# Transposing x, q and k of batches 2 to 4 by DMA instead of on TensorE, in a fused attention and mixing kernel

## The chip, the cores and the metric

One NeuronCore of a Trainium2 chip. The time is device microseconds (us) of one execution. TensorE multiplies matrices, VectorE (DVE in the profile) and ScalarE (ACT) work element by element, GpSimd (POOL) does the same more slowly, SyncE (SP) only issues transfers. All transfers go through 16 DMA engines that the issuers share. An execution counts as slow when it is over 1.5% above the fastest of its kernel. Ratios below use fast runs alone, with a 95% interval.

## The reference

```python
# q, k, v: (4 batches, 8 heads, 768 tokens, 64), f32; heads 0, 2 and 6 are "retrieval" heads
scores = q @ k.T / 8
# retrieval heads: causal mask; the others: 4 first tokens, and a window of 64 tokens
a = softmax(where(mask, scores, -1e9))
x = (a @ v).transpose(0, 2, 1, 3).reshape(4, 768, 512)
theta = x @ w_theta
zr, zi = x * cos(theta), x * sin(theta)
y = w_tok_r @ zr + w_tok_i @ zi          # mixes the tokens, per batch
u = x + y
out = u + maximum(u @ w_ch, 0)
```

## The kernel before

Matrix products run in bf16. Three operands have to be turned so that the contracted axis lies on the partitions: q and k (head dimension) before the scores, and x (channels) before theta. Before the change TensorE turns all of them: two heads at a time into a PSUM tile, from which a copy takes them to SBUF. The copies also order the tokens, because a partition of the loaded tile holds six neighbouring tokens.

```python
def load_qk(what, b, heads):             # f32 in DRAM, bf16 in SBUF: a casting load, issued by POOL
    if (what, b) not in state:
        state[what, b] = two.tile([128, H, NB * D], BF16, tag=f"{what}b", name=f"{what}b")
    src = {"q": q, "k": k}[what][b].rearrange("h (p j) d -> p h (j d)", p=128)
    nc.gpsimd.dma_start(out=state[what, b][:, heads], in_=src[:, heads])

def load_v(b, n, after=None):            # not cast: issued by SP, in two halves per pair of heads
    ...
    for x, h in enumerate(PAIRS[n]):
        nc.sync.dma_start(out=t[:, x], in_=src[:, h])

def turn_qk(what, b, n):                 # 12 transposes: 6 token blocks of 2 heads
    pt = state["pt", what, n] = ps_x.tile([128, 1024], BF16, tag="x", name="pt")
    for j in range(NB):
        for x, h in enumerate(PAIRS[n]):
            nc.tensor.transpose(pt[64 * x:64 * x + 64, j * 128:(j + 1) * 128], state[what, b][:, h, j * D:(j + 1) * D], ident)

def keep_qk(eng, what, n):               # PSUM to SBUF, tokens ordered
    o = dst.rearrange("d (p j) -> d p j", j=NB)
    i = state.pop(("pt", what, n))[:, :S].rearrange("d (j p) -> d p j", j=NB)
    ...

def turn_x(b, i):                        # 4 transposes of a 128-token tile of x; keep_x copies them out
    ...
```

The order of instructions on every engine is not the order of the code. A small planner holds a list of steps, each with an engine, an estimated duration and what it depends on. It simulates them and emits every engine's queue in the simulated order. A transfer is a step with an estimated landing time:

```python
tp = add("PE", 340, lambda ...: turn_qk(what, b, n), [landed[what, b, n]], take="x", mode="64c")
kept[what, b, n] = add("ACT" if act else "DVE", 720 if act else 900, lambda ...: keep_qk(...), [tp] + old, give=[tp])
...
issue = add("SP", 1500, lambda b=b, n=n: load_v(b, n), [cast[b - 1, n], xk[b - 1, 5]], take="st_v")
land = add("DMA", 2000, None, [issue])
```

On the chip each queue runs strictly in that order. A step whose input is late holds up all that stands behind it, needed or not. Batches are counted from 1 in the text and from 0 in the code.

The softmax here doesn't subtract the row's maximum and nothing guards it: scores larger than these inputs give would overflow.

Of the kernel before, what the change touches and what calls it, by code (L numbers as in the profile page):

```python
# [10 lines left out]
BF16 = mybir.dt.bfloat16  # L11
# [6 lines left out]
PAIRS = [(0, 2), (4, 6), (1, 3), (5, 7)]  # L18
# [13 lines left out]
class Plan:  # L32
# [5 lines left out]

    LATENCY = {"PE": (230, 0), "ACT": (190, 60), "DVE": (120, 60), "POOL": (150, 60), "SP": (50, 0), "DMA": (2000, 0)}
    SWITCH = {"PE": 95, "ACT": 1300}  # L40
# [13 lines left out]
    def order(self, free):  # L54
# [4 lines left out]
        rank = {}  # L59
# [21 lines left out]
        while events:  # L81
# [8 lines left out]
            for e in engines:  # L90
# [3 lines left out]
                for s in ready.get(e, ()):  # L94
                    if ready_at[id(s)] > now or (s.take and slots[s.take] < 1):
                        continue
                    value = -ready_at[id(s)] if e == "DMA" else rank[id(s)] + s.bias
                    if s.mode and s.mode != mode.get(e):
                        value -= self.HOLD.get(e, 0)
                    if best is None or value > best[0]:  # L100
                        best = (value, s)
# [32 lines left out]
def kernel(  # L134
# [28 lines left out]
    two = ctx.enter_context(tc.tile_pool(name="two", bufs=2))  # L163
    stage = ctx.enter_context(tc.tile_pool(name="stage", bufs=4))
    work = ctx.enter_context(tc.tile_pool(name="work", bufs=2))
# [28 lines left out]
    state = {}  # L194
    plan = Plan({"s": 2, "m": 2, "x": 2, "u": 4, "uT": 3, "ot": 2, "ct": 2, "st": 2, "wtok": 4, "st_v": 4})
    add = plan.add
# [7 lines left out]
    def load_qk(what, b, heads):  # L204
        if (what, b) not in state:
            state[what, b] = two.tile([128, H, NB * D], BF16, tag=f"{what}b", name=f"{what}b")
        src = {"q": q, "k": k}[what][b].rearrange("h (p j) d -> p h (j d)", p=128)
        nc.gpsimd.dma_start(out=state[what, b][:, heads], in_=src[:, heads])
# [38 lines left out]
    def turn_qk(what, b, n):  # L247
        pt = state["pt", what, n] = ps_x.tile([128, 1024], BF16, tag="x", name="pt")
        for j in range(NB):
            for x, h in enumerate(PAIRS[n]):  # L250
                nc.tensor.transpose(pt[64 * x:64 * x + 64, j * 128:(j + 1) * 128], state[what, b][:, h, j * D:(j + 1) * D], ident)  # L251

    def keep_qk(eng, what, n):
# [164 lines left out]
    def turn_x(b, i):  # L418
        pt = state["ptx", b, i] = ps_x.tile([128, 1024], BF16, tag="x", name="pt")
        for kk in range(KD):  # L420
            nc.tensor.transpose(pt[:, kk * 128:(kk + 1) * 128], state["x", b][:, i, kk * 128:(kk + 1) * 128], ident)  # L421

    def keep_x(b, i):
        (nc.scalar.copy if b == 0 else nc.vector.tensor_copy)(state["xT", b][:, :, i * 128:(i + 1) * 128], state.pop(("ptx", b, i))[:, :DM].rearrange("p (k t) -> p k t", k=KD))
# [120 lines left out]
    landed = {}  # L545
    gate = [add("DMA", ns, None) for ns in (2600, 2400, 4800)]
    for n in range(4):
# [4 lines left out]

    turned, kept, sinkk, scored, sunk, cast, shift = {}, {}, {}, {}, {}, {}, {}
    av, norm, xt, xk, th, zs, ud, ch = {}, {}, {}, {}, {}, {}, {}, {}
# [16 lines left out]

    def turn_steps(b):
        for n in range(4):
            for what in "qk":
                old = []
                if b:
                    old = [s for key, s in scored.items() if key[0] == b - 1 and key[1] == n] + ([sunk[b - 1][0]] if n else [])
                    if what == "k" and n:
                        old.append(sinkk[b - 1, n])
                tp = add("PE", 340, lambda what=what, b=b, n=n: turn_qk(what, b, n), [landed[what, b, n]], take="x", mode="64c")  # L580
                act = (what == "q" and n < 2) or (b > 0 and (what == "q" or n < 2))
                kept[what, b, n] = add("ACT" if act else "DVE", 720 if act else 900, lambda act=act, what=what, n=n: keep_qk("ACT" if act else "DVE", what, n), [tp] + old, give=[tp])
            if n:
                sinkk[b, n] = add("POOL", 250 * (1 if n == 1 else 2), lambda n=n: sink_keys(n), [kept["k", b, n]] + ([sunk[b - 1][0]] if b else []))

    def v_steps(b):
        for n in range(4):
            if b == 0:
                issue = add("DVE", 200, lambda n=n: load_v(0, n, kT[n // 2]), [kept["k", 0, n // 2]], take="st_v")
                land = add("DMA", 2000, None, [issue])  # L590
            else:
                issue = add("SP", 1500, lambda b=b, n=n: load_v(b, n), [cast[b - 1, n], xk[b - 1, 5]], take="st_v")
                land = add("DMA", 2000, None, [issue])
            old = [s for key, s in av.items() if key[0] == b - 1] if b else [cleared[1]]
            cast[b, n] = add("DVE" if b == 0 else "POOL", 570 if b == 0 else 830, lambda b=b, n=n: cast_v(nc.gpsimd if b else nc.vector, b, n), [land] + old, give=[issue])
            for x, h in enumerate(PAIRS[n]):
                if not IS_RETR[h]:
                    shift[b, h] = add("POOL", 960, lambda b=b, n=n, x=x: shift_v(nc.gpsimd, b, n, x), [cast[b, n]], give=[issue])

    def attention_steps(b):  # L600
# [25 lines left out]
        for i in range(NB):  # L626
# [12 lines left out]
            old = [ud[b - 2, t] for t in range(NB)] if b > 1 else []  # L639
            norm[b, i] = add("DVE", 850, lambda b=b, i=i: normalize(b, i), [av[b, i]] + old, give=[av[b, i]])  # L640
            xt[b, i] = add("PE", 224, lambda b=b, i=i: turn_x(b, i), [norm[b, i]], take="x", mode="128")
            old = [th[b - 1, t, y] for t in (0, 2, 4) for y in range(2)] if b else []
            xk[b, i] = add("DVE" if b else "ACT", 400 if b else 480, lambda b=b, i=i: keep_x(b, i), [xt[b, i]] + old, give=[xt[b, i]])
# [14 lines left out]
    def mlp_steps(b):  # L658
        for t in range(NB):
# [8 lines left out]
            st = add("SP", 100, lambda b=b, t=t: store(b, t), [fin])  # L668
            add("DMA", 900, None, [st], give=[fin])

# [15 lines left out]

    load_steps(1, [])
    weights(2, 2, [])
# [5 lines left out]
    sink_done = []  # L694
    for half in range(2):
        first = add("SP", 500, lambda half=half: sink_values(2 * half), [cleared[2]] + sink_done)
        land = add("DMA", 100, None, [first])
        sink_done.append(add("DVE", 480, lambda half=half: nc.vector.tensor_copy(vs[:32, 2 * half:2 * half + 2, :, :D], vs_f), [land, cleared[3], ones_done]))
    attention_steps(0)
    for b in range(1, B):  # L700
        turn_steps(b)
        v_steps(b)
        if b + 1 < B:
            load_steps(b + 1, [kept[what, b - 1, n] for what in "qk" for n in range(4)])
        attention_steps(b)
        mlp_steps(b - 1)
# [46 lines left out]
```

## Time and profile before

| | before |
|---|---|
| median of 3 runs | 226.41 us (226.37 to 229.37) |
| profiled span | 227.5 us, mean TensorE clock 0.971 of full speed |
| busy: TensorE / VectorE / ScalarE / POOL | 195.2 / 122.2 / 120.2 / 101.1 us |
| packets of SP's transfer queue, share of the 16 engines' time | 28,664, 21.2% |

The prediction below shows the slices and the chain.

The timeline of the kernel before (start, length, engine, line, operation) has the first scores of batch 2 in this stretch:

```profile
63.68 0.85 PE L322 MATMUL ps<-qT,kT 64*128 64x384 bf16 x19
```

### The profile page before, as it was taken

Reading aid. Unit: us, or ns where it says so; the run is one execution under the profiler, and the core shown is the slowest. Engines: PE = TensorE matmul, PEld = TensorE weight load, DVE = VectorE, ACT = ScalarE, POOL = GpSimd, SP = SyncE. Lnnn points to the kernel's source line nnn. Section 1 sums busy time; section 2 is a strip of 40 time slices with the busy share of each in tenths; the row PEclk is TensorE's granted clock in tenths of the full one; section 3 lists DMA queues with packets and bytes.
Section 4 is the critical chain, followed back from the end, with each engine's and each line's share of the span. In section 5 each row is a group of like instructions: output and inputs, shape, how many; then the busy total and the mean of one; then the engine's idle time right before and its main releaser. Section 6 shows DMA issues by size and latency. Waiting matters only on the chain.

```text
span 227.5 us, 5040 instructions
## 1 busy us (share of the span) xinstructions
PE 195.2 (86%) x2124; PEld 113.1 (50%) x2124; DVE 122.2 (54%) x203; ACT 120.2 (53%) x156; POOL 101.1 (44%) x180
## 2 busy tenths in 40 slices
PE   0688549968997899999999999959999999689990
PEld 0555339634554577544553468525544575234440
DVE  6327815389542168479135168495451764974341
ACT  2477402793499960184777563644977526703120
POOL 7955992072488300349852200299835000780000
PEclk9999999999999589999999999997999999999997
DMA  6994599999994934902103000960012000210303
GB/s 76 164 210 108 80 174 213 192 200 199 195 209 98 202 55 118 208 14 81 49 0 127 14 0 3 242 178 0 3 48 94 3 3 0 92 49 0 138 0 140
DMA packets 39759, 22.63 MB, mean 99 GB/s; under 512 B 25912, under 2 KB 36664, under 8 KB 39736
## 3 DMA queue, kind: packets, MB, share of 16 engines
q0 software_dynamic: 11072, 9.70, 27.4%
q1 hardware_dynamic: 28664, 12.61, 21.2%
q8 instruction: 16, 0.26, 0.5%
q14 instruction: 7, 0.06, 0.1%
HBM read 25.71 MB, written 6.29 MB: 141 GB/s over the span
## 4 chain that ended last, share of the span: by engine, by line
PE 72%; DVE 8%; ACT 6%; DMA 5%; POOL 3%; issue 3%; POOLq 1%; SPq 1%; DVEq 0%; ACTq 0%
PE py L455 26%; PE pav L409 9%; PE ps L322 9%; PE pc L474 7%; PE pt L251 7%; PE ps L432 6%; DVE zr L442 5%; POOL zi L445 3%; PE pt L421 3%; PE pt L464 3%; DMA vs_f<-in_v_dram 2%; PE pt L494 2%; DMA kb<-in_k_dram 2%; ACT P L341 2%; ACT P_st L338 1%
## 5 line engine op out<-in xcount | busy, mean ns | idle before, releaser
L455 PE MATMUL py<-zr,wtokTr 128*128 128x512 bf16 x144 | 39.7, 385 | 6.3 <-DVE zr L442 6.3
L445 POOL TENSOR_TENSOR zi<-x,st 128x512 bf16<-128x512 bf16 x20 | 27.8, 1421 | 25.2 <-ACT st L439 19.8
L455 PE MATMUL py<-zi,wtokTi 128*128 128x512 bf16 x144 | 38.5, 379 | 0.1
L459 DVE TENSOR_TENSOR u<-x,py 128x512 bf16<-128x512 bf16 x24 | 16.5, 687 | 36.1 <-PE py L455 36.1
L322 PE MATMUL ps<-qT,kT 64*64 64x128 bf16 (+6 forms) x380 | 26.7, 266 | 6.5 <-ACT P L341 2.2
L442 DVE TENSOR_TENSOR zr<-x,ct 128x512 bf16<-128x512 bf16 x24 | 27.9, 1197 | 1.3 <-ACT ct L437 1.3
L468 ACT COPY uT<-pt 128x512 bf16<-128x512 bf16 x24 | 13.9, 586 | 26.5 <-PE pt L464 26.4
L478 DVE SCALAR_TENSOR_TENSOR ot<-pc,u 128x512 f32<-128x512 f32 x24 | 16.5, 688 | 16.4 <-PE pc L474 15.1
L222 POOL CAST vt<-st_v 128x768 bf16<-128x768 f32 x12 | 10.2, 856 | 33.3 <-DMA st_v<-in_v_dram 33.1
L322 PEld LDWEIGHTS <-kT 64*64 64x64 bf16 (+1 forms) x380 | 13.6, 113 | 21.7 <-issue 17.1
L200 POOL TENSOR_SCALAR_AFFINE_SELECT P<-P 128x256 bf16<-128x256 bf16 (+1 forms) x48 | 16.5, 365 | 17.2 <-ACT P L346 6.6
L474 PE MATMUL pc<-w_ch_sb,uT 128*128 128x512 bf16 x96 | 24.0, 380 | 0.0
L432 PE MATMUL ps<-w_theta_sb,xT 128*128 128x512 bf16 x96 | 23.2, 379 | 0.9 <-ACT st L439 0.9
L437 ACT ACTIVATE ct<-ps,half_pi 128x1024 f32<-128x1024 f32 x12 | 13.0, 1113 | 20.1 <-PE ps L432 19.5
L341 ACT ACTIVATE P<-ps 128x1024 bf16<-128x1024 f32 (+2 forms) x24 | 21.2, 923 | 4.5 <-PE ps L322 4.5
L455 PEld LDWEIGHTS <-wtokTr 128*128 128x128 bf16 x144 | 12.6, 98 | 19.7 <-issue 7.6
L258 ACT COPY qT<-pt 128x768 bf16<-128x768 bf16 x14 | 11.0, 802 | 18.7 <-PE pt L251 18.5
L455 PEld LDWEIGHTS <-wtokTi 128*128 128x128 bf16 x144 | 13.3, 98 | 14.9 <-issue 0.4
L358 DVE TENSOR_TENSOR P_st<-P_st,m_stream 128x512 bf16<-128x512 bf16 (+2 forms) x24 | 12.8, 543 | 14.7 <-ACT P_st L349 10.5
L409 PE MATMUL pav<-vx,P_st 128*128 128x65 bf16 x120 | 17.4, 207 | 3.5 <-POOL vx L228 3.5
L409 PE MATMUL pav<-vt,P 128*128 128x65 bf16 x252 | 16.1, 207 | 1.8 <-DVE x L416 1.8
L409 PE MATMUL pav<-vt,P_st 128*128 128x65 bf16 x120 | 17.5, 208 | 0.0
(73 smaller groups left out, 323.8 us busy)
## 6 DMA issues: line engine op xcount, KB each, us to landing
st_v<-in_v_dram SPq DMA_DIRECT2D x32, 192.0 KB
out_dram<-ot SPq DMA_DIRECT2D x24, 256.0 KB
qb<-in_q_dram POOLq DMA_DIRECT2D x3, 768.0 KB, 10.8
kb<-in_k_dram POOLq DMA_DIRECT2D x3, 768.0 KB, 15.4
wtok<-in_moe_w_tok_r_dram POOLq DMA_DIRECT2D x3, 384.0 KB, 11.9
wtok<-in_moe_w_tok_i_dram POOLq DMA_DIRECT2D x3, 384.0 KB, 12.7
w_theta_sb<-in_moe_w_theta_dram POOLq DMA_DIRECT2D x1, 512.0 KB, 5.7
w_ch_sb<-in_moe_w_ch_dram POOLq DMA_DIRECT2D x1, 512.0 KB, 21.1
```

The lines of the kernel that those rows point to most:

```text
L200: nc.gpsimd.affine_select(out=t, in_=t, compare_op=ALU.is_ge, fill=0.0, base=base, pattern=pattern, channel_multiplier=cm)
L251: nc.tensor.transpose(pt[64 * x:64 * x + 64, j * 128:(j + 1) * 128], state[what, b][:, h, j * D:(j + 1) * D], ident)
L322: nc.tensor.matmul(ps[half, yy, c:c + w], l, r, start=True, stop=True, skip_group_check=True)
L341: nc.scalar.activation(P.rearrange("p (y c) -> p y c", y=2), ps[:, :, :w0], AF.Exp, scale=scale)
L409: nc.tensor.matmul(o, l, r, start=(m == 0), stop=True, skip_group_check=True)
L432: nc.tensor.matmul(ps[:, y], state["xT", b][:, kk, (i + y) * 128:(i + y + 1) * 128], w_theta_sb[:, kk], start=(kk == 0), stop=(kk == KD - 1))
L442: nc.vector.tensor_tensor(state["zr", b][:, i + y], state["x", b][:, i + y], state["ct", b, i][:, y], ALU.mult)
L445: (nc.vector if eng == "DVE" else nc.gpsimd).tensor_tensor(state["zi", b][:, i + y], state["x", b][:, i + y], state["st", b, i][:, y], ALU ...
L455: nc.tensor.matmul(py, wtokT[n][:, s, t * 128:(t + 1) * 128], z[:, s], start=(g == 0 and m == 0), stop=(g == 2 and m == 3))
L459: nc.vector.tensor_tensor(u, state["x", b][:, t], state.pop(("py", b, t)), ALU.add)
L474: nc.tensor.matmul(pc, uT[:, kk], w_ch_sb[:, kk], start=(kk == 0), stop=(kk == KD - 1))
L478: nc.vector.scalar_tensor_tensor(ot, state.pop(("pc", b, t)), 0.0, state.pop(("u", b, t)), ALU.max, ALU.add)
```

## The change

The intent: take 288 transposes of q and k and 72 of x off the fullest engine and let the DMA crossbar do them. The new code lays both heads of a pair side by side, which VectorE does first (`pair_qk`), and sends them as one transpose. It delivers the tokens in the loaded order, so a strided copy on ScalarE, VectorE or POOL orders them at the end (`spread_qk`). All DMA transposes are issued by SP. Smaller edits came along: one buffer instead of two for loaded q and k, three `st_v` buffers instead of four, half of the sink values loaded later, batch 1's value shifts on VectorE, and other estimates.

```diff
-    stage = ctx.enter_context(tc.tile_pool(name="stage", bufs=4))
+    stage = ctx.enter_context(tc.tile_pool(name="stage", bufs=3))
...
-            state[what, b] = two.tile([128, H, NB * D], BF16, tag=f"{what}b", name=f"{what}b")
+            state[what, b] = two.tile([128, H, NB * D], BF16, tag=f"{what}b", name=f"{what}b", bufs=1)
...
+    def pair_qk(what, b, n):
...
+        nc.vector.tensor_copy(state["qp", what, b][:, n], state[what, b][:, h0:h1 + 1:h1 - h0].rearrange("p x (j d) -> p j x d", d=D))
+    def send_qk(what, b, n):
+        t = state["pt", what, n] = work.tile([128, NB, 128], BF16, tag="raw", name="raw", bufs=3)
+        nc.sync.dma_start_transpose(t, state["qp", what, b][:, n].rearrange("p j x d -> p (j x d)"))
+    def spread_qk(eng, what, n):
+        o = dst.rearrange("d (p j) -> d p j", j=NB)
+        i = state.pop(("pt", what, n)).rearrange("d j p -> d p j")
...
+    def send_x(b, i):
+        nc.sync.dma_start_transpose(state["xT", b][:, :, i * 128:(i + 1) * 128], state["x", b][:, i])
...
+                if b:
+                    issue = add("SP", 1100, lambda ...: send_qk(what, b, n), [paired[what, b, n]], take="raw")
+                    land = sent[what, b, n] = add("DMAH", 1000, None, [issue])
+                    eng = "ACT" if what == "q" and n < 2 else "POOL" if n > 1 and what == "k" else "DVE"
+                    kept[what, b, n] = add(eng, 850, lambda ...: spread_qk(eng, what, n), [land] + old, give=[issue])
+                    continue
...
+            if b:
+                issue = add("SP", 800, lambda b=b, i=i: send_x(b, i), [norm[b, i]] + old)
+                xk[b, i] = add("DMAH", 900, None, [issue])
+                continue
...
-            load_steps(b + 1, [kept[what, b - 1, n] for what in "qk" for n in range(4)])
+            load_steps(b + 1, [paired[what, b, n] for what in "qk" for n in range(4)])
```

## The prediction

> **What bounds the kernel now.** I read the 40 slices of the span first, to see which engine is full where.
>
> ```profile
> PE   0688549968997899999999999959999999689990
> DVE  6327815389542168479135168495451764974341
> PEclk9999999999999589999999999997999999999997
> DMA  6994599999994934902103000960012000210303
> ```
>
> One slice is 5.7 us. TensorE is thin for nine slices (to about 51 us), then nearly full to slice 34 (about 190 us) with one hole in slice 26; the last seven slices are the last batch's MLP. DMA is full in the first 65 us and almost idle after 95 us, apart from slices 25 and 26. Busy time in chosen windows gives that in numbers; the columns after the window are its length, then busy us and count for PE, PEld, DVE, ACT and POOL, the TensorE clock, the DMA share and GB/s.
>
> ```profile
> 24.00:34.00 10.00, 5.17 (x54) 3.65 (x53) 4.75 (x10) 1.78 (x4) 9.55 (x15) 1.00 0.89 142
> 34.00:45.00 11.00, 10.40 (x146) 8.82 (x147) 4.94 (x11) 5.14 (x8) 1.55 (x3) 1.00 1.27 203
> 55.00:104.00 49.00, 45.98 (x542) 27.79 (x540) 25.68 (x48) 30.46 (x42) 20.85 (x40) 0.93 0.76 139
> 104.00:154.00 50.00, 47.06 (x547) 25.71 (x545) 29.27 (x49) 29.58 (x38) 23.01 (x37) 0.99 0.26 75
> 154.00:191.00 37.00, 36.75 (x457) 21.14 (x456) 18.93 (x35) 23.08 (x31) 14.63 (x32) 0.97 0.06 23
> 191.00:205.00 14.00, 11.47 (x52) 4.81 (x51) 10.37 (x11) 5.98 (x6) 9.01 (x6) 1.00 0.15 57
> ```
>
> From 55 to 191 us TensorE is busy 129.8 of 136 us (45.98 + 47.06 + 36.75), 95%; no other engine passes 62%. So there the time is TensorE's work, and work taken from it should shorten the span. From 24 to 34 us it is half idle while POOL is busy 9.55 of 10. The chain of work that ended last shows what else held that stretch, and what a batch's turn costs later (start, duration, what):
>
> ```profile
> 25.71 0.68 DVE vs L698
> 27.75 5.37 DMA vs_f<-in_v_dram
> 33.85 0.70 DVE x L416
> ...
> 104.23 0.81 PE pt L251 x24
> 105.47 0.96 DVE kT L260
> 107.00 0.97 PE py L455 x4
> 107.97 0.79 PE pt L251 x24
> ```
>
> The first three lines are a wait for the sink values of batches 3 and 4, which nobody needs yet: the copy sits in VectorE's queue ahead of the first normalization, which therefore starts at 33.6 us. The later ones show 24 transposes of q or k in 0.81 us, lying on the chain.
>
> **What the Trainium skill says.** "TensorE: Matmul & The Clock Gate", Part 4: PE-mode transpose, gives about 390 ns for a 128x128 bf16 transpose in isolation and about 275 ns in a kernel. This trace has 219 ns as the duration of one, but 24 in 0.81 us, so 34 ns each as issued: the saving must be counted at the issue rate, not at durations. "VectorE: DVE Perf Modes", The three transpose paths, gives 1309 ns for a 128x128 crossbar transpose by DMA against 390 ns for TensorE; so each single transpose gets slower and the change pays only if it is hidden. "DMA: Bandwidth & Descriptors", Latency and other measured facts, gives 261 GB/s for a DMA transpose with a non-contiguous middle dimension, and its Anatomy section about 2 us of fixed cost. No run before shows a DMA transpose.
>
> **The change part by part.**
>
> **1. TensorE loses work.** Three batches of 96 q/k transposes are 288; at 34 ns they take 9.7 us. The x transposes of those batches are 18 tiles of four. The timeline:
>
> ```profile
> 187.96 0.39 PE L421 MATMUL pt<-ident,x 128*128 128x128 bf16 x4
> 188.18 1.03 PE L432 MATMUL ps<-w_theta_sb,xT 128*128 128x512 bf16 x4
> ```
>
> The next group starts 0.22 us later, so 18 x 0.22 = 4.0 us. Sum 13.7 us, 4.6 us per batch of about 49 us. As TensorE is 95% full there, and some of what is removed will turn into waiting, I count 10 us of it.
>
> **2. The copies move.** The rows concerned (busy us, mean ns, idle before):
>
> ```profile
> L258 ACT COPY qT<-pt 128x768 bf16<-128x768 bf16 x14 | 11.0, 802 | 18.7 <-PE pt L251 18.5
> L260 DVE COPY kT<-pt 128x768 bf16<-128x768 bf16 x10 | 9.2, 949 | 4.5 <-PE pt L251 4.5
> L424 DVE COPY xT<-pt 128x512 bf16<-128x512 bf16 x18 | 7.2, 419 | 5.3 <-PE pt L421 5.3
> ```
>
> ScalarE drops from 6 to 2 such copies per batch: 12 x 0.8 = 9.6 us less. But the instruction order of the changed kernel has 12 activation table loads instead of 8, at 1.28 us each: 5.1 us back. VectorE loses 6 x 0.95 + 18 x 0.42 = 13.3 us and gains 24 interleaving copies (estimate 0.4 us, below the 0.55 us of a 128x768 copy out of PSUM) and 12 strided ones (estimate 0.9 us, as L260): 20.4 us. That is +7 us over three batches, 2.4 us per batch on an engine with over 20 us free in each. POOL gains 6 spreads of some 0.9 us in batches 2 to 4 and loses the five value shifts of batch 1. None of these becomes the bound.
>
> **3. SP and DMA.** 24 transposes of 192 KB and 18 of 128 KB, all from SP, so no two streams transpose at once. By the skill's figures one of 192 KB is estimated at 2 + 197 KB / 261 GB/s = 2.8 us from issue to landing. The plan in the diff reckons 1.1 us of SP and some 3 us to landing. With three raw buffers a pair takes about 1.1 + 3 + 0.9 = 5 us, so eight need some 14 us of a 49 us batch: hidden, as long as the instruction order is right. The x path gets longer by about 3 us per tile (send and land 3.8 us against 0.22 on TensorE plus 0.42 on VectorE and hand-overs). The new TensorE order covers it: after the last attention values of batch 4 it still has 24 mixing matmuls of batch 3 (5.2 us) placed between the theta matmuls, where the old order had none.
>
> **4. Not named in the few words, but in the diff.** The second half of the sink values moves to batch 2, and the value shifts of batch 1 move from POOL (0.5 and 0.46 us each) to VectorE. This takes away the 5.2 us wait at 28 us and the waits of TensorE on L228. First normalization near 28.5 instead of 33.6 us: 5 us at that place. But DMA is full from 34 to 65 us (share 1.2 to 1.3 with overlap), and batch 2's q and k, the token weights and v all come through it. What POOL issues earlier (about 4 us) lands earlier; I count 4 us.
>
> **5. What comes back.** In batch 2 the transposes stand on SP behind eight v loads, in the stretch where DMA is full. The new TensorE order does only 8 mixing matmuls before batch 2's first scores, against 36 in the old, so a late transpose leaves TensorE with nothing to do. I take off 2 us.
>
> Sum: 226.4 - 10 - 4 + 2 = 214.4 us.
>
> **The rivals.**
> **(a) A wait takes the place of the work.** If landing takes 5 to 6 us instead of 3, the spreads in the in-order queues of VectorE, ScalarE and POOL hold back u, ot and masks, and SP holds x behind q and k. For: DMA share over 1.2 till 65 us, four kinds of transfer in one SP queue. Against: DMA share 0.06 to 0.26 from 104 to 191 us. It would eat half or all of part 1: 219 to 226 us.
> **(b) TensorE's work was not the bound as much as it looks**, and table loads, exponentials (ScalarE was busy 9.8 of 10 us from 65 to 75 us) or the zr/zi pair of VectorE and POOL at each batch's end set the pace. For: the hole at 146 to 153 us, with both of them nearly full. Against: only 6 us of such holes from 55 to 191 us. 217 to 221 us.
> **(c) All of it is gained**: the removed 13.7 us in full and 5 us at the start, and the hole at 150 us is filled because the next scores are ready earlier. 206 to 209 us.
>
> **Range and chances.** I hold the sum most likely and give (a) and (b) together more weight than (c): 214.5 us, 205 to 223 us in 8 of 10. Faster by over 2% means below 221.9 us: 0.81. Within 2%: 0.13. Slower: 0.06, which needs transposes of over 6 us each, or a queue that stands still behind them.
>
> **What the changed profile would show.** Right: 1764 matmuls instead of 2124, TensorE's busy time from 195 to some 180 us and still over 90% between the first scores of batch 2 and the last values; first normalization before 30 us and no wait on vs_f there; transposes landing in 3 to 4 us; the last output tile in the same relation to the last values as before (36 us). Wrong: waits of the L269, L271 and L273 copies, or of SP, on raw that sum to over 10 us; TensorE idle for over 5 us just before batch 2's scores; theta (L457) waiting on xT. The prediction fails upward if a DMA transpose occupies SP or the DMA engines for several us, for then 42 of them do not fit beside the v loads and stores; it fails downward if the start gains more than 4 us.

## More of the kernel before

What matters later is the stretch where batch 2 begins, so here is the busy time in three windows there. The columns are the window, its length, the busy us (and count) of TensorE, its weight loads, VectorE, ScalarE and POOL, then the TensorE clock, the DMA share and GB/s.

```profile
45.00:55.00 10.00, 7.08 (x51) 3.76 (x49) 8.63 (x10) 7.01 (x9) 5.47 (x6) 1.00 1.20 198
55.00:65.00 10.00, 9.89 (x141) 5.73 (x140) 5.42 (x9) 5.28 (x9) 4.43 (x12) 1.00 1.24 198
65.00:75.00 10.00, 8.00 (x87) 4.38 (x88) 3.10 (x5) 9.81 (x14) 9.05 (x19) 0.98 0.80 147
```

TensorE is nearly full from 55 to 65 us, and at the same time the DMA engines are full too (share above 1 means overlapping packets).

## The result, and the profile after

| | before, same rounds | after |
|---|---|---|
| median | 227.82 us (226.37 to 229.37, 4 runs) | 247.88 us (247.24 to 248.66, 4 runs) |
| profiled span, mean TensorE clock | 227.5 us, 0.971 | 246.5 us, 0.894 |
| busy: TensorE / VectorE / ScalarE / POOL | 195.2 / 122.2 / 120.2 / 101.1 us | 182.8 / 128.1 / 120.5 / 109.5 us |
| packets of SP's transfer queue, share | 28,664, 21.2% | 57,656, 40.4% |

The ratio is 1.0881 [1.0774, 1.0987]. Here and below a ratio compares the fast runs of two kernels in the same rounds, so it is not quite the ratio of the medians, which count all runs. The change made the kernel 20 us slower, although TensorE works 12.4 us less.

The 40 slices of the kernel after (6.2 us each) show where:

```profile
PE   1696858320509999909955898999569999999992
PEclk9999879965576999986995699999998999999999
DMA  5999999999999057997991018776200044020203
```

Slices are counted from 1 here. TensorE has a hole from slice 8 to 12 (about 43 to 74 us), one in slice 18 (105 to 111 us) and a half one in slices 21 and 22. In the first hole the clock falls, and the DMA row is full all along. The windows of the kernel after, columns as before:

```profile
45.00:55.00 10.00, 3.66 (x22) 1.64 (x23) 6.73 (x11) 2.64 (x3) 5.43 (x7) 0.79 1.24 189
55.00:65.00 10.00, 1.29 (x4) 0.47 (x4) 2.29 (x3) 4.35 (x5) 4.84 (x5) 0.50 1.13 88
65.00:75.00 10.00, 3.28 (x42) 2.25 (x41) 2.23 (x4) 2.65 (x4) 1.81 (x2) 0.67 1.29 185
...
105.00:115.00 10.00, 3.53 (x9) 1.24 (x10) 1.99 (x3) 0.00 (x0) 2.01 (x4) 0.69 1.19 192
```

In the 30 us where TensorE had worked 24.97 us (7.08 + 9.89 + 8.00) it now works 8.23 us, and no other engine takes over. They all wait. From 55 to 65 us the transfers move 88 GB/s where they had moved 198, at about the same share: each packet stands longer in its engine. The waits of the kernel after say for what (total us, times, longest):

```profile
POOL kT L271 <- DMA raw<-kp: 19.0, 4, 9.9
DVE kT L273 <- DMA raw<-kp: 17.4, 3, 9.3
...
PE py L480 <- DVE zr L467: 15.6, 4, 11.3
...
ACT qT L269 <- DMA raw<-qp: 12.6, 1, 12.6
...
DVE qT L273 <- DMA raw<-qp: 10.2, 1, 10.2
...
PE ps L457 <- DMA xT<-x: 7.1, 1, 7.1
...
PE ps L344 <- POOL kT L271: 6.7, 1, 6.7
```

The copies that order q and k wait 59.2 us in all for the transposes, on three engines. TensorE waits 6.7 us for one of these copies. It waits more, 11.3 us at once, for `zr`, which has nothing to do with q or k. The timeline of the kernel after tells why (idle time before, and what ended it, in brackets; SPq is SP's issuing):

```profile
43.23 14.47 SPq L262 DMA_TRANSPOSE raw<-qp  x3
...
51.05 0.68 DVE L467 TENSOR_TENSOR zr<-x,ct 128x512 bf16<-128x512 bf16 x1
...
60.65 2.88 ACT L269 COPY qT<-raw 128x768 bf16<-128x768 bf16 x2 [12.59 <-DMA raw<-qp]
61.97 1.09 DVE L273 COPY qT<-raw 128x768 bf16<-128x768 bf16 x1 [10.24 <-DMA raw<-qp]
62.15 8.35 SPq L262 DMA_TRANSPOSE raw<-kp  x3
62.98 0.67 DVE L467 TENSOR_TENSOR zr<-x,ct 128x512 bf16<-128x512 bf16 x1
63.70 2.29 PE L480 MATMUL py<-zr,wtokTr 128*128 128x512 bf16 x5 [11.34 <-DVE zr L467]
...
72.48 1.47 POOL L271 COPY kT<-raw 128x768 bf16<-128x768 bf16 x1 [9.94 <-DMA raw<-kp]
...
74.00 0.86 PE L344 MATMUL ps<-qT,kT 64*64 64x64 bf16 x26 [6.72 <-POOL kT L271]
```

VectorE did a `zr` at 51.05 us and the next at 62.98 us. Between them in its queue stands the copy of batch 2's q, which waits 10.24 us for its transpose. ScalarE stands 12.59 us in front of two such copies. So batch 1's token mixing stops for batch 2's transposes. When q has landed, the same happens with k, and batch 2's first scores start at 74.00 us against 63.68 before.

The page does not give the landing times of these transposes. I worked them out from the trace's DMA packets: every q or k transpose is 768 packets of 256 bytes, so the packets of SP's queue can be counted off against the issues. All 55,376 came out even (the 57,656 of the table without 2,280 packets of 4 bytes). The counting takes the 16 engines together, so where some engines lag it gives a transpose's last packet too early. The trace also has the semaphore updates by which each transfer reports that it is complete; the last column has the time from issue to the last of these, and it is this that the copies wait for. For the first eight transposes of batch 2 and one in a quiet stretch:

```
transpose  issued  SP busy  first packet  last packet  issue to last  to completion
q          43.23   4.92     53.59         57.14        13.91 us       17.39 us
q          48.20   5.87     56.87         60.65        12.45          13.07
q          54.17   3.54     60.63         61.47         7.31           7.77
k          62.15   1.63     66.37         71.30         9.15          10.27
k          63.95   1.93     71.24         73.93         9.98          10.66
k          65.99   4.51     73.90         74.73         8.74           9.37
k          73.97   1.22     75.15         77.97         4.00           5.33
q          76.84   1.21     78.02         79.16         2.32           2.89
quiet (k) 147.45   1.21    148.63        149.48         2.03           2.50
```

In a quiet stretch a transpose of q or k takes 2.03 us to its last packet, 0.86 us of it moving packets. In batch 2 it takes up to 13.91 us, and 17.39 us to completion: ScalarE's first copy of q starts at 60.65 us, just after the first transpose completes at 60.62. The time has two parts: waiting for the first packet, and packets that crawl. Below, the times of transposes are those counted off to the last packet; completion came 0.4 to 3.5 us after it in the transposes of batch 2 here. The two v loads issued at 38.6 and 39.0 us completed only at 49.3 and 57.6, so the first part is the queue: the q transposes stand behind batch 2's v on SP. The second part shows in the packets per half microsecond (number, mean ns of one):

```
us          POOL's casting loads   SP's queue
52.5-53.0   58 of 131 ns           56 of  31 ns   (v)
57.0-57.5    7 of 134              60 of 206      (q transpose)
58.5-59.0    3 of 134              64 of 179      (q transpose)
60.5-61.0    0                    552 of  18      (q transpose)
69.5-70.0   95 of  78              91 of  34      (k transpose)
74.0-74.5    0                    469 of  21      (k transpose)
```

Beside a full load the two queues alternate nearly one packet to one (95 and 91), and the load's packets are the larger ones: 768 to 1,536 bytes in the trace against 256. The Trainium skill, "DMA: Bandwidth & Descriptors", Queues, rings and completion order, says that an engine "round-robins between the queue rows it has work for, at *packet* granularity", and these counts fit that. (The page's packet is a bundle of some 9 to 17 descriptors; the trace shows pieces of 256 to 1,536 bytes and not the bundles, so the grain of the alternation is not shown.) A transpose in small packets so loses most of the bandwidth: 552 packets in half a microsecond alone, 91 beside a load. The rows at 57 and 58.5 us were new to me: the load is down to 3 to 7 packets of 134 ns in half a microsecond, which is one or two of 16 engines, and the transpose is even slower, at 60 to 64 packets of 179 to 206 ns. It gets to 18 ns when the load's last packets are gone. That reads as if a transpose went at the pace of its slowest engine; the trace shows that the two end together, and no run tests the reason.

The hole of slice 18 has the same look one batch later. POOL issues the loads of batch 4's q and k at 96.43 and 97.32 us; two k transposes of batch 3 and an x tile of batch 2 between them, issued from 97.55 to 101.48 us, then take 9.8, 11.1 and 9.9 us, and TensorE's theta waits 7.1 us for x.

The lower clock goes with it, and what it costs was not measured by itself. The Trainium skill, "TensorE: Matmul & The Clock Gate", Part 1, has the array fall to half its clock after an idle window of some 3.4 us, and the 0.50 of the window from 55 to 65 us agrees. The mixing matmuls rose from a mean of 385 and 379 ns to 402 and 409 ns.

### The profile page after: what moved, and what is told of

Same layout as the page of the kernel before. It is cut to its first block, busy times and chain, and to the rows that moved or that the text cites. A ratio compares the mean times of both kernels' runs of the same rounds, so it can differ in the third digit from the quotient of the medians.

```text
span 246.5 us, 4398 instructions
## 1 busy us (share of the span) xinstructions
PE 182.8 (74%) x1739; PEld 98.2 (40%) x1764; DVE 128.1 (52%) x225; ACT 120.5 (49%) x148; POOL 109.5 (44%) x176
## 3 DMA queue, kind: packets, MB, share of 16 engines
q1 hardware_dynamic: 57656, 19.69, 40.4%
## 5 line engine op out<-in xcount | busy, mean ns | idle before, releaser
L480 PE MATMUL py<-zi,wtokTi 128*128 128x512 bf16 x137 | 40.9, 409 | 1.8 <-issue 0.9
L470 POOL TENSOR_TENSOR zi<-x,st 128x512 bf16<-128x512 bf16 x20 | 26.0, 1320 | 24.1 <-PE py L480 20.9
L200 POOL TENSOR_SCALAR_AFFINE_SELECT P<-P 128x256 bf16<-128x256 bf16 (+1 forms) x48 | 18.8, 410 | 30.7 <-ACT P L366 10.9
L457 PE MATMUL ps<-w_theta_sb,xT 128*128 128x512 bf16 x94 | 24.9, 400 | 9.2 <-DMA xT<-x 7.1
L462 ACT ACTIVATE ct<-ps,half_pi 128x1024 f32<-128x1024 f32 x12 | 13.3, 1115 | 30.3 <-PE ps L457 28.5
L222 POOL CAST vt<-st_v 128x768 bf16<-128x768 f32 x12 | 11.7, 978 | 28.4 <-DMA st_v<-in_v_dram 16.0
L467 DVE TENSOR_TENSOR zr<-x,ct 128x512 bf16<-128x512 bf16 x24 | 23.0, 987 | 2.4 <-ACT ct L462 2.4
L360 ACT ACTIVATE P_st<-ps 128x512 bf16<-128x512 f32 (+1 forms) x16 | 12.5, 809 | 13.0 <-PE ps L344 13.0
L271 POOL COPY kT<-raw 128x768 bf16<-128x768 bf16 x6 | 9.2, 1531 | 21.0 <-DMA raw<-kp 19.0
L457 PEld LDWEIGHTS <-xT 128*128 128x128 bf16 x96 | 9.3, 100 | 20.5 <-DMA xT<-x 8.2
L438 DVE TENSOR_TENSOR x<-pav,r 128x512 bf16<-128x512 f32 x24 | 16.6, 691 | 0.9
```

The lines of the kernel that those rows point to most:

```text
L200: nc.gpsimd.affine_select(out=t, in_=t, compare_op=ALU.is_ge, fill=0.0, base=base, pattern=pattern, channel_multiplier=cm)
L360: nc.scalar.activation(stream_out(banks[0][1], 2, q0, w), ps[:, :, :w].rearrange("p s (c x) -> p s c x", x=64), AF.Exp, scale=scale)
L438: nc.vector.tensor_tensor(dst, av[:, :, :, :D], r.unsqueeze(3).to_broadcast([128, 2, 4, D]), ALU.mult)
L457: nc.tensor.matmul(ps[:, y], state["xT", b][:, kk, (i + y) * 128:(i + y + 1) * 128], w_theta_sb[:, kk], start=(kk == 0), stop=(kk == KD - 1))
L467: nc.vector.tensor_tensor(state["zr", b][:, i + y], state["x", b][:, i + y], state["ct", b, i][:, y], ALU.mult)
L470: (nc.vector if eng == "DVE" else nc.gpsimd).tensor_tensor(state["zi", b][:, i + y], state["x", b][:, i + y], state["st", b, i][:, y], ALU ...
```

## The experiments

Eighteen kernels ran, in five groups. Most of them build on the kernel after, through two switches that say which batches take the DMA way; everything else of the change stays in:

```diff
+    DMA_QK, DMA_X = (1, 2, 3), (1, 2, 3)     # batches 2 to 4, counted from 0
-        if b:                                 # q and k, in two places
+        if b in DMA_QK:
-            if b:                             # x
+            if b in DMA_X:
-  load_steps(b + 1, [paired[what, b, n] for ...])
+  load_steps(b + 1, [paired[what, b, n] if b in DMA_QK else turned[what, n] for ...])
```

A time below is the median of all runs of a kernel, slow ones included; a ratio is to the kernel before on the same chip and in the same rounds. The eighteen were measured in five sets, each on another chip, so times of different sets compare only roughly. Taken at 2% from the kernel before, one is clearly faster (x alone), four are slower, three the same and ten unclear; gains of 1 to 3% below are readings near the noise. In the set of four runs (v behind, weights behind, measured times for x, and x with the smaller edits) only two of seven runs of the kernel before count as fast, 224.19 and 227.17 us, and their intervals are wide.

Two theories stood at the start. **Batch 2's transposes**: they meet v, token weights and loads, and nearly all of the loss comes from there. **The rival**: the added work itself (copies, table loads, SP issues of 1.2 us each) costs in every batch.

### Which part of the change

**All transposes back on TensorE**, which leaves the smaller edits:

```diff
+    DMA_QK, DMA_X = (), ()
```

> The changed kernel with all its other edits (one q and one k buffer, three v buffers, value shifts on VectorE, second half of the sink values late, new estimates in the plan), but every transpose on TensorE again. Theory C (the DMA transposes of batch 2, and less of batch 3, land late because plain loads that cast run on the same DMA engines): 221 to 229 us, as nothing is left to land late. Rival S (the side edits and the new order cost the time): 235 us or more.

Measured: 227.87 us, ratio to before 0.9994 [0.9914, 1.0074]. The smaller edits together neither gain nor lose. This kernel is the base line for the next ones.

**x alone by DMA:**

```diff
+    DMA_QK, DMA_X = (), (1, 2, 3)
```

> Only x of batches 2 to 4 goes by DMA transpose; q and k are on TensorE. Theory C: x of batch 2 still meets the load of q and k of batch 4, a few us at one place, against 4 us of TensorE work saved: 220 to 230 us. Rival L (any DMA transpose costs latency on the path, wherever it stands): 230 us or more.

Measured: 221.62 us, 0.9691 [0.961, 0.9771]; 6.3 us less than the base line on the same chip.

**Only batch 2 by DMA**, q, k and x:

```diff
+    DMA_QK, DMA_X = (1,), (1,)
```

> q, k and x by DMA transpose in batch 2 alone, batches 3 and 4 on TensorE. Theory C: nearly the whole loss comes from here: 238 to 248 us, with TensorE idle for over 15 us between 45 and 75 us. Rival E (the strided copies of 1.5 us on ScalarE and POOL and the extra table loads, alike in each batch): a third of the 20 us, so 231 to 235 us.

Measured: 245.72 us, 1.0769 [1.0684, 1.0854]; 17.8 us more than the base line, most of the 20 us. The windows of this kernel, columns as above:

```profile
45.00:55.00 10.00, 1.49 (x15) 0.98 (x16) 2.68 (x4) 0.00 (x0) 6.33 (x10) 0.83 1.28 141
55.00:65.00 10.00, 0.00 (x0) 0.00 (x0) 0.81 (x1) 4.59 (x5) 0.10 (x1) 0.50 1.36 129
65.00:75.00 10.00, 3.57 (x17) 1.91 (x16) 3.43 (x6) 0.48 (x1) 0.00 (x0) 0.50 1.37 155
```

TensorE does nothing at all for 10 us. Worked out as above, the first three q transposes took 17.8, 17.8 and 14.2 us, the first three of k 9.9, 10.7 and 7.1 us.

**Only batches 3 and 4 by DMA:**

```diff
+    DMA_QK, DMA_X = (2, 3), (2, 3)
```

> q, k and x by DMA transpose in batches 3 and 4, batch 2 on TensorE. Theory C: 220 to 231 us; issue to last packet 2 to 4 us in batch 4, longer in batch 3 where the load of q and k of batch 4 runs. Rival E: two thirds of the loss, 237 to 242 us.

Measured: 226.26 us, 0.9881 [0.9785, 0.9976] (only its times are compared). These two batches do not lose, although the first k transpose of batch 3 took 13.65 us and the next 6.15: late by itself is not yet lost time. The place of the loss is settled: batch 2.

### Why the transposes of batch 2 are late

What lies beside them comes from three sources: the loads of the next q and k, the v loads, and the token and channel weights. These runs take them away in turn.

**No loads of q and k for batches 3 and 4**, the tiles of batch 2 being used again:

```diff
-        nc.gpsimd.dma_start(out=state[what, b][:, heads], in_=src[:, heads])
+        if b < 2:
+            nc.gpsimd.dma_start(out=state[what, b][:, heads], in_=src[:, heads])
+        else:
+            state[what, b] = state[what, 1]
```

> Wrong result on purpose: the changed kernel with the loads of q and k for batches 3 and 4 left out, batch 2's data is turned again; order and work of the engines unchanged. Theory C: the k transposes of batch 2 and the late ones of batch 3 land in 2 to 4 us instead of 9 to 11, first scores of batch 2 near 66 us instead of 74, the hole before theta of batch 2's x (105 to 111 us) gone: 230 to 239 us. The q transposes of batch 2 still meet the token weights and stay slow. Rival O (the plan's order alone is at fault): the loads do not matter, 244 us or more.

Its output is wrong, which doesn't matter for the time. The comparison does not see which batch's q and k are used. Measured: 232.53 us, 1.0202 [1.0098, 1.0306]; 15 us less than the kernel after. The k transposes of batch 2 took 2.03 to 2.04 us instead of 9 to 10, those of q still 16.1, 13.3 and 7.7 us, and the first scores of batch 2 came 7.7 us earlier:

```profile
66.31 0.53 PE L347 MATMUL ps<-qT,kT 64*64 64x64 bf16 x26
```

This edit is outside the plan: by the traces VectorE, ScalarE and SP run the same instructions in the same order as in the kernel after, and only the four load issues are gone from POOL. So the order is no rival here: k was late because of the loads, q because of something else.

**The same loads deferred** until the transposes have landed, which keeps the result right:

```diff
-            load_steps(b + 1, [paired[what, b, n] for what in "qk" for n in range(4)])
+            load_steps(b + 1, [sent[what, b, n] for what in "qk" for n in range(4)])
```

> The changed kernel with one edit: the load of the next batch's q and k stands after the landing of this batch's transposes in the plan, not after the interleaving copies. Same work and traffic. Theory C: k of batch 2 lands 4 to 8 us earlier and batch 3 loses its waits: 231 to 241 us. Rival O or E: 244 us or more.

Measured: 234.90 us, 1.0348 [1.0271, 1.0424], 13 us less than the kernel after (the plan is new with this edit, so the order changes too); k at 2.03 to 3.50 us, q at 14.4, 14.1 and 8.5 us. The windows of this kernel show the hole that q leaves:

```profile
45.00:55.00 10.00, 2.52 (x14) 1.71 (x16) 3.41 (x8) 0.10 (x1) 3.66 (x4) 0.51 1.18 199
55.00:65.00 10.00, 3.78 (x21) 2.06 (x22) 4.37 (x7) 6.49 (x6) 0.00 (x0) 0.50 0.72 104
```

**Also v of batch 2 behind the transposes.** This asks whether q is late because it stands behind v on SP's queue, or because it shares the engines with the weights:

```diff
-  issue = add("SP", 700, ...load_v(b, n), [cast[b - 1, n], xk[b - 1, 5]], take="st_v")
+  issue = add("SP", 700, ...load_v(b, n), [cast[b - 1, n], xk[b - 1, 5]] + ([sent[what, b, m] for what in "qk" for m in range(4)] if b == 1 else []), take="st_v")
```

> e7 (loads of the next q and k deferred, 234.9 us) with one more edit: batch 2's eight value loads stand on SP behind batch 2's q and k transposes instead of ahead of them. In e7 the first transpose waits 9 us from issue to its first packet behind those value loads, and then shares the engines with the token weights. Theory Q (the queue is the larger part): first packets some 6 to 9 us earlier, 225 to 230 us. Theory W (sharing with the casting loads is the larger part): transposes still take 5 us or more each, 231 us or more.

Measured: 234.63 us, 1.0384 [1.0202, 1.0565]; no gain over the run before. The first q packet came at 42.87 us instead of after v, but the transposes still took 9.75, 11.35 and 8.62 us, beside 121 to 182 KB per us of POOL's loads, channel and token weights for the most part. The queue in front was only part of it: for the first q 14.4 us became 9.75.

**Also the channel weights and the last token weights behind the transposes:**

```diff
-    (w_ch load, then weights(4, 2, []))              # ahead of batch 1's attention
+        if b == 1:
+            issue = add("POOL", 780, ...w_ch..., last_pool + [sent[what, 1, n] for what in "qk" for n in range(4)])
+            ...
+            weights(4, 2, [])
```

> e13 with w_ch and the last token weights also loaded after batch 2's q and k transposes. Theory Q and W together: batch 2's transposes near the 2.0 us of a quiet stretch once the earlier loads have landed, 218 to 227 us, and TensorE over 6 us busy in 45 to 55 us. Rival O (late token weights or values now hold the mixing): 228 us or more with waits on wtok or st_v.

Measured: 229.63 us, 1.0141 [0.9929, 1.0353]. The first q transposes of batch 2 took 4.9, 4.4 and 3.8 us, the rest of that batch mostly 2.04. The windows of this kernel show the hole nearly closed:

```profile
45.00:55.00 10.00, 8.18 (x47) 3.87 (x47) 7.85 (x13) 7.49 (x8) 1.81 (x4) 0.83 0.63 93
55.00:65.00 10.00, 9.21 (x108) 4.75 (x111) 3.91 (x8) 8.39 (x13) 8.18 (x17) 1.00 1.11 203
```

This is the sum of the story: 247.9 to 234.9 us with the next loads out of the way, no change with v, 229.6 us with the weights. Some 17 of the 20 us are gone by the ratios (1.0881 to 1.0141), with all transposes still on DMA. What is left is not better than before, as the rival had it (228 us or more, with waits on v): v and the weights now come later (POOL waits 27.9 us for v), the first two q transposes of batch 3 take 7.6 and 7.1 us, and the gain on TensorE does not show. The weights behind without v behind was not run, so how the two divide is open; and each of these runs has its own order, so the share of the last step, some 5 us, is less sure than that of the loads.

### The planner's part

**A landing time of 7 us in the plan**, for batch 2's transposes, nothing moved by hand. If the waits come only from a plan that believes in 1 us, the right estimate should cure them:

```diff
-  land = sent[what, b, n] = add("DMAH", 1000, None, [issue])
+  land = sent[what, b, n] = add("DMAH", 1000 if b > 1 else 7000, None, [issue])
```

> The changed kernel with one number of the plan changed: a DMA transpose of batch 2 is reckoned to land 9 us after its issue instead of 3, so other work is put ahead of what waits for it. Rival O (right traffic, wrong order): 224 to 232 us. Theory C with a bandwidth that cannot be planned around, since the q and k of batch 2 are late whatever the order: 238 to 248 us.

Measured: 244.87 us, 1.0741 [1.065, 1.0831]. The windows of this kernel:

```profile
55.00:65.00 10.00, 9.65 (x51) 4.63 (x52) 2.73 (x5) 4.98 (x6) 0.00 (x0) 0.71 1.52 167
...
85.00:95.00 10.00, 5.13 (x48) 2.52 (x48) 4.70 (x11) 8.12 (x12) 3.35 (x10) 0.65 0.26 59
```

From 55 to 65 us TensorE is busy 9.65 instead of 1.29 us: mixing no longer stops behind the copies. But it only spends the mixing earlier. From 75 to 115 us TensorE works 23.5 of 40 us (7.09 + 5.13 + 7.30 + 3.98). The first scores of batch 2 come at 78.33 us, later than the 74.00 of the kernel after, with no wait in front of them: the first k transpose still takes 9.33 us, and the new order has put mixing ahead of the scores. So a truer estimate moved the wait and did not remove it; how much of what is left is the order and how much the late data, this run does not tell.

**A landing time of 12 us in the plan for batch 2's v**, on the kernel with x alone by DMA, as v does land that late:

```diff
-                land = add("DMAH", 2000, None, [issue])
+                land = add("DMAH", 12000 if b == 1 else 2000, None, [issue])
```

> e2 (x alone by DMA) with one estimate of the plan changed: batch 2's values are reckoned to land 14 us after issue instead of 4, as e2's trace shows. Theory: the 5 us in which TensorE waits near 50 us for ScalarE, ScalarE for zi on POOL and POOL for those values goes, 214 to 219 us. Rival: the next late load takes its place, 220 us or more.

Measured: 234.96 us, 1.0292 [1.0215, 1.0369]: 13 us more than with 2 us in the plan. A miss, and a warning: one estimate, with no work added or removed, moved the time as far as the loads did.

**Measured times in the plan for x**, 1.22 us on SP and landing soon after:

```diff
-  issue = add("SP", 800, ...send_x...);  xk[b, i] = add("DMAH", 900, None, [issue])
+  issue = add("SP", 1220, ...send_x...); xk[b, i] = add("DMAH", 100, None, [issue])
```

> e2 (x alone) with the plan's two numbers for an x transpose set to what the traces show: 1.22 us of SP, 0.1 + 2 us to landing. Nothing else. This also measures how much the order that the plan happens to find is worth: if within 1.5 us of e2's 221.6 us, the differences of several us among e8, e11 and e12 are effects of their edits; if 3 us or more apart, they may be the order alone.

Measured: 222.78 us, 0.9879 [0.9714, 1.0044], within 1.2 us of the other estimates by the medians, though on another chip; by the ratios (0.9879 and 0.9691) the two lie 1.9% apart, within the wide interval. No effect of these numbers is shown, and none of 4 us is ruled out.

### What the DMA way is worth where nothing is late

**x in batches 2 to 4, q and k in batch 4 alone**, which has no next load:

```diff
+    DMA_QK, DMA_X = (3,), (1, 2, 3)
```

> x of batches 2 to 4 by DMA transpose, and q and k of batch 4 alone, which no plain load accompanies. Theory C: x alone gave 221.6 us; 3.2 us of TensorE's work less: 216 to 221 us. Rival E (strided copies and interleaving cost more than TensorE's transposes even in a quiet stretch): 222 us or more.

Measured: 222.11 us, 0.9783 [0.9706, 0.9861]; all its transposes took 1.8 to 3.6 us. Two of its four runs are slow; the fast ones took 219.38 and 221.41 us. Against x alone (0.9691, other chip) no gain from 96 transposes less on TensorE shows.

**The same with a needless load beside batch 4's transposes**, to price a late landing by itself:

```diff
+        if b + 1 == B:                       # loads q and k of batch 4 once more, after the interleaving
+            for what in "qk":
+                issue = add("POOL", 900, ...load_qk(what, b, slice(0, 8)), [paired[k] for k in paired if k[1] == b] + last_pool, bias=-20000)
```

> e8 with the suspected cause put in: as soon as batch 4's q and k are interleaved they are loaded once more into the same two buffers (nobody reads them; the result stays right), as the changed kernel does with the next batch's. Theory C: batch 4's transposes that fall beside these loads take 5 to 14 us to their last packet instead of 2 to 4, and the kernel gets 3 us or more slower than e8 (222.1 us in its rounds). Rival (the loads are harmless, batch 2 is slow for another reason): transposes at 2 to 4 us and within 1.5 us of e8.

Measured: 223.24 us, 0.9726 [0.9639, 0.9812]. Three transposes rose to 5.7, 4.0 and 4.8 us, and the time did not. A miss: landings of up to 5.7 us cost nothing that shows here. TensorE was busy 11.78 of the 12 us from 124 to 136 us, where they fall, so it had other work ready in its order. That batch 2 paid because its transposes were later and more stood behind them fits this, but no run varies the two apart.

**x in batches 2 to 4, q and k in batches 3 and 4, loads deferred:**

```diff
+    DMA_QK, DMA_X = (2, 3), (1, 2, 3)
-  load_steps(b + 1, [paired[what, b, n] if ...])
+  load_steps(b + 1, [sent[what, b, n] if ...])
```

> x of batches 2 to 4, and q and k of batches 3 and 4, by DMA transpose, with batch 4's load after the landing of batch 3's transposes. Theory C alone: another 6.4 us of TensorE work less than e2: 214 to 219 us. With rival E (even in a quiet stretch the interleaving and strided copies give back what TensorE saves, as e8 hints): 219 to 225 us.

Measured: 225.12 us, 0.9847 [0.9785, 0.991]. Its transposes took 1.8 to 3.8 us, and it is slower than x alone.

**q and k in batches 3 and 4 alone, loads deferred, x on TensorE:**

```diff
+    DMA_QK, DMA_X = (2, 3), ()
...                                      # and the deferred loads as above
```

> q and k of batches 3 and 4 by DMA transposes, x of all batches on TensorE, next loads of q and k deferred until the transposes have landed; the rest as in the run with all transposes back on TensorE (227.9 us). Theory: the copies, waits and table loads that come with q and k give back what TensorE saves, 226 to 231 us. Rival: q and k gain their 192 transposes of 34 ns, 6.5 us, when nothing lies beside them: 223 us or less, and then the loss in the runs with x is from the two together.

Measured: 222.82 us, 0.9741 [0.9675, 0.9808], against 0.9994 for the base line without transposes. The rival was right and I was wrong: q and k do gain by themselves, some 2.5%, near the 6.5 us of TensorE work taken away. So the copies and waits of the DMA way do not eat the gain wherever they stand, and why it is missing in the runs that have x by DMA as well stays open.

### The smaller edits, and x without them

**The late half of the sink values and batch 1's value shifts, in the kernel before:**

```diff
-                    shift[b, h] = add("POOL", 960, ...shift_v(nc.gpsimd, b, n, x), ...)
+                    shift[b, h] = add("POOL" if b else "DVE", 960 if b else 340, ...)
...
+        if b == 1:
+            sink_steps(1, [sink_done[0], cast[1, 0]])      # the second half: no longer ahead of batch 1
```

> The kernel before with two of the side edits alone: the second half of the sink values fetched in batch 2, and batch 1's value shifts on VectorE. My prediction counted 4 us for them: 222 to 225 us. Rival D (the start is paced by the loads, so what is earlier waits for the token weights): 225 to 229 us.

Measured: 226.94 us against 228.59, 0.9894 [0.981, 0.9979]. By the fast runs this is worth 2.4 us, with an interval of 0.5 to 4.3 us: less than the 4 us that I had counted is likely, but 4 us is not excluded.

**The same, and x by DMA:**

```diff
-            xt[b, i] = add("PE", 224, ...turn_x(b, i), [norm[b, i]], take="x", mode="128")
+            if b:
+                issue = add("SP", 800, lambda b=b, i=i: send_x(b, i), [norm[b, i]] + old)
+                xk[b, i] = add("DMA", 900, None, [issue])
+                continue
```

> e10 (the kernel before with the two side edits, 226.9 us) with x of batches 2 to 4 by DMA transpose, double q and k buffers and the old estimates kept. Theory: the x part is worth 4 to 6 us wherever it stands, 220 to 223 us. Rival (e2's gain was the luck of its order): 225 us or more.

Measured: 219.58 us, 0.9708 [0.9513, 0.9903]. It and the kernel with x alone on the changed base (221.62 us, 0.9691) are the fastest, better than both kernels.

**x by DMA in the kernel before, and nothing else:**

> Kernel before with x of batches 2 to 4 by DMA transposes and no other edit. Theory: x is worth some 7 us by itself (the run of the side edits went from 226.9 to 219.6 with it), so 219 to 224 us here. Rival: it needs the late half of the sink load or the value shifts, then 225 us or more.

Its edit is the one just shown, without the two ahead of it. Measured: 229.15 us, 0.9936 [0.9846, 1.0026]. A miss. TensorE is busy 188.5 us, 6.7 less than before, and the span is not shorter. The planner's order has 16 activation table loads of 1.28 us here, against 8 before and 10 in the run just above, so ScalarE switches between exponential and sine twice as often. That this is the reason was not tested.

What these last runs leave, as far as readings near the noise go: x is worth 2 to 3% in two settings and nothing in a third; q and k of batches 3 and 4 are worth 2.5% alone and nothing on top of x. Each of these runs has its own order on every engine. So the gain of an edit whose worth is 4 to 7 us does not look like a property of the edit alone here; that it depends on the order which the planner finds with it is likely and was not tested by itself. How much of it is table loads, and how much where TensorE happens to stand idle, stays open.

## Why the prediction was wrong

**What failed** is step 5, "What comes back". It saw the place and the mechanism: batch 2's transposes "stand on SP behind eight v loads, in the stretch where DMA is full", with only 8 mixing matmuls ahead of the scores, and said that "a late transpose leaves TensorE with nothing to do". It put 2 us on this. The run with batch 2 alone has 17.8 us, and that is net of what TensorE saves there. The term was mis-sized for two reasons that the runs showed. The landing time came from figures for a lone transpose, 2.8 us. Alone that held: 2.50 us to completion, 2.03 us to the last packet (the 2 us of fixed cost are on a page section about transfers that GpSimd issues; SP issued these). The first six of batch 2 took 7 to 14 us to the last packet, 8 to 17 us to completion, so part 3's "eight need some 14 us" became 35.9 us from the first issue (43.23) to the last packet (79.16). And the wait was put on TensorE's scores alone, where the copies of late data stopped VectorE and ScalarE, and batch 1's mixing with them.

**Missed altogether**: the edit of the next loads' start. Part 3 calls the transposes "hidden, as long as the instruction order is right", but the order lets POOL load the next q and k exactly while they are in flight. Taking these loads away with the order unchanged brings 15 of the 20 us back, deferring them 13. The diff showed that line.

**Rival (a)** had the right kind of loss with 5 to 6 us for a landing, and so stopped at 226 us. The condition given for slower, "transposes of over 6 us each, or a queue that stands still behind them", is what happened, at a chance of 0.06. Its argument against, that DMA share is "0.06 to 0.26 from 104 to 191 us", spoke for batches 3 and 4, where indeed little was lost. It did not speak for batch 2, at a share of 1.2.

**Part 1**, TensorE's work: the count held, 1,764 weight loads instead of 2,124 (the trace has 1,739 of the matmuls, some records being lost), and busy time fell to 182.8 us against "some 180". That 10 of 13.7 us would be gained did not hold as a sum. On the changed base x alone brought 6.3 us and q and k of two batches about 2.5%; together less than either, and x alone in the kernel before nothing.

**Part 2**, the copies: interleaving took 0.35 to 0.46 us (estimated 0.4) and VectorE's strided copies 0.8 to 0.9 us (estimated 0.9). ScalarE took 1.57 us and POOL 1.53 us for the same copy, where the prediction had 0.8 and 0.9. That is 4.6 us more on ScalarE over six copies (6 x 0.77), on an engine that was not the bound. Twelve table loads came as told.

**Part 4**, the smaller edits: the first normalization came at 28.39 us, as predicted (28.5). But the run of the two edits alone priced them at 2.4 us (0.5 to 4.3), and in the run with all smaller edits together (0.9994) no gain is left.

**The signs named in advance** all showed the wrong way (the prediction counts its slices 25 and 26 from 0, the others from 1, which changes no reading): waits on raw of 59.2 us (limit 10), TensorE idle for 6.7 and 11.3 us ahead of batch 2's scores (limit 5), theta waiting 7.1 us on xT.

## What to carry to other kernels

Before moving work to the DMA engines, price it in the busiest stretch where it will run, with the transfers that run there, not by its time alone; a transpose in small packets took up to seven times its lone time here, counted from issue, with its wait in the queue. Look at what the change itself starts at that moment: a buffer freed earlier may release a load into the very transfers that freed it. Where queues run in a planned order, a late input stops unrelated work behind it, and an edit of a few microseconds should be judged under more than one order, as the same edit gained 3% or nothing.

## What the Trainium skill lacked or had wrong

- "DMA: Bandwidth & Descriptors", Latency and other measured facts, has 261 GB/s for a transpose. Alone it came out somewhat lower: 197 KB in 0.86 us is 229 GB/s; 2.03 us from issue to last packet, 2.50 us to completion. It lacks what happens beside other transfers: 9 to 10 us beside casting loads, and 206 ns per packet instead of 18 while a load's last packets drain on one or two engines.
- "Advanced Engine Details and Errata", X-Bar Transpose (TRN2), says that transposes "are as fast as regular DMAs". In this trace they move in packets of 256 bytes, and beside a load that has packets of 768 bytes they got 40 KB per us against its 135. Alone the statement is near: 0.85 us for the 768 packets of a transpose, 0.71 to 0.74 us for the 768 of a v load at its quickest (119.1 and 120.5 us).
- No page that I looked at gives the time in us for which a transpose holds SP (one table has cycles, for "previous generations"): here 1.20 to 1.24 us, for 128 KB and for 192 KB alike, and up to 5.87 us with the queue full.
- "VectorE: DVE Perf Modes", The three transpose paths, has 1309 ns for a 128x128 block. Six such blocks in one transfer took 2.03 us, so the figure cannot be multiplied by the number of blocks; the page does not say so.
- "TensorE: Matmul & The Clock Gate", Part 4, has 275 to 390 ns for a transpose, as a duration. As issued here, 24 took 0.81 us, 34 ns each, and it is this that work taken away should be counted by.
- No page that I looked at gives the cost of the copy with stride that follows: 128x768 bf16 in SBUF took 0.8 to 0.9 us on VectorE, and 1.57 and 1.53 us on ScalarE and POOL.
